# Step one of a two-step Fourier transform on TensorE: 128-row products with a zero-padded table against 64-row products per channel half

## The chip, the cores and the metric

The kernel runs on one core of one Trainium2 chip. A core has a matrix engine (TensorE, "PE" in the profile, with its weight loads as "PEld"), a vector engine (VectorE, DVE), a scalar engine (ScalarE, ACT), GpSimd (POOL) and a sync engine (SP) that here only issues DMAs. The engines run their own instruction streams and wait for each other through semaphores. SBUF is the working memory, 128 partitions wide; TensorE writes its results to PSUM, eight banks of 512 fp32 values per partition.

The metric is the device time of one execution in microseconds (us). The kernel before took 699.45 us in the median of three runs (695.64 to 699.81).

## The reference, cut to what matters

An H3 block (with adaptive layer norm) is followed by a token-mixing MLP. The change touches only the long convolution of the H3 block:

```python
kv = k_shift * v                                    # (S, D), S = 2048, D = 640
kv_f = rfft(pad(kv, S));  kf_f = rfft(pad(ssm_k, S))
y = irfft(kv_f * kf_f)[:S] + kv * ssm_D
out = q * y
```

`k_shift` is a causal convolution over four tokens, done on VectorE and GpSimd. After the convolution come a second layer norm and the MLP (2048 to 1728 to 2048 over the token axis), which make up the larger part of the time.

## The kernel before, in words

The 640 channels are worked in five chunks of 128 (loop variable `c`, L511). Each chunk has two halves of 64 channels, called `h`; tokens are split as n = 32 n1 + n2, with n1 (64 values) on the partitions. So partitions 0 to 63 hold the 64 n1 of the first channel half and partitions 64 to 127 those of the second.

The transform of each chunk has two steps forward and two back:

- **step1** (L210): 64-point transform over n1. It is called for two sides, the signal (side 0, in tile `x`) and the filter (side 1, in tile `p`), and for four values of t, each with eight pairs of channels (`a`). One `pst` tile (two PSUM banks, 1024 columns) holds one t. ScalarE copies it into the spectrum tile `z` (L220). The stationary operand is a 128 x 64 slice of the data; the moving operand is a column block of the table F1 (L218).
- **f2** (L223): 32-point transform with twiddles, stationary w, moving `z`, eight groups g, two column halves of the array. The product of signal and filter spectrum follows on ScalarE (L237: copy of the filter part to `kt`), VectorE (L242, L244: products into `p`, through the helper L59) and GpSimd or VectorE (L250: sums into `y`).
- **i2** (L254) and **i1** (L273): the two inverse steps. i2 works on 32-row tiles of the array and is copied back into `z` by ScalarE (L271, four copies); i1 works on 64 x 64 tiles, four of them, and its result is multiplied on VectorE with the normalised query (`gate`, L302, writes `aux`).

Nothing is scheduled by a planner: the order of the program text is the order on each engine. For a middle chunk TensorE's order is: f2 of the eight groups; step1(0,0), step1(0,1) of the next chunk; i2(0); step1(0,2); i2(1); step1(0,3); i1(0); step1(1,0); i1(1); step1(1,1) to step1(1,3); then f2 of the next chunk. Chunk 0 is set up ahead of the loop (L486 to L492), and in the last chunk there is no step1. Between the f2 groups VectorE is given the short convolution of the chunk after next (`fill`, `dv`; tiles `tap`, `kt`, `x`) or, late, statistics for the second layer norm (L510, tile `sm`).

The `pst` tiles are a ring of three (`ring`, L67: slots 0, 1, 2), shared by step1, f2, i2 and i1; a fourth pair of banks is the tile `tap`. A product of TensorE in fp32 appears in the trace as two pairs of a weight load and a matmul: the 16 products written in one step1 call are 32 such pairs.

The tables come from `_constants` (L21). F1 has a row for each (h, n1) and, for cosine and sine, a column for each (k1, h); it is zero where the two h differ, so that one 128-row product gives both halves at once, side by side. The tables F1, V2 and a unit matrix are loaded together as `SM` (L454, 420 columns).

Of the kernel before, what the change touches and what calls it, by code (L numbers as in the profile page):

```python
# [11 lines left out]
AF = mybir.ActivationFunctionType  # L12
# [8 lines left out]
def _constants():  # L21


    n1, n2, k1, k2 = np.arange(64), np.arange(32), np.arange(64), np.arange(32)
    a = 2 * np.pi * ((1 + 4 * k1)[None, :] * n1[:, None] % 256) / 256
    f1 = np.zeros((2, 64, 2, 64, 2))
    for h in range(2):
        f1[h, :, 0, :, h], f1[h, :, 1, :, h] = np.cos(a), np.sin(a)
    ang = 2 * np.pi * ((1 + 4 * k1)[None, :, None] * n2[:, None, None] / 8192
                       + (k2[None, None, :] * n2[:, None, None] % 32) / 32)  # L30
    w2 = np.zeros((2, 32, 2, 64, 2, 2, 32))
    for c in range(2):
        w2[0, :, c, :, 0, c] = np.cos(ang)
        w2[1, :, c, :, 0, c] = -np.sin(ang)
        w2[0, :, c, :, 1, c] = np.sin(ang)
        w2[1, :, c, :, 1, c] = np.cos(ang)
    ang = 2 * np.pi * (k2[:, None] * n2[None, :] % 32) / 32
    c, s = np.cos(ang), np.sin(ang)
    v2 = np.tile(np.concatenate([c, -s, s, c], 1), (4, 1))
    ang = 2 * np.pi * ((1 + 4 * k1)[:, None, None] * (32 * n1[None, None, :] + n2[None, :, None]) % 8192) / 8192  # L40
    v1 = np.tile(np.stack([np.cos(ang), np.sin(ang)], 1).reshape(64, 4096) / 2048, (2, 1))
    sel = np.zeros((128, 128))
    sel[0, 0:64] = sel[1, 64:128] = 1
    small = np.concatenate([f1.reshape(128, 256), v2, np.eye(128)[:, 0:36], sel], 1)
    return {"small": small.astype(np.float32), "w2": w2.reshape(128, 8192).astype(np.float32),
            "v1": v1.astype(np.float32)}

# [2 lines left out]
def mixer_kernel(ctx: ExitStack, tc: tile.TileContext, q, k, v, shift_k, ssm_k, ssm_D, w1, b1, w2, b2, c,  # L50
# [24 lines left out]
    def dram(t, offset, ap):  # L75
        return bass.AP(tensor=t.tensor, offset=t.offset + offset, ap=ap)
# [15 lines left out]
    KT = [T_kt[:, 512 * i:512 * i + 512] for i in range(2)]  # L92
    TV = T_kt[:, 1024:1536].rearrange("p (n i) -> p n i", i=64)

    Z = T_z.rearrange("p (s k t a e) -> p s t a k e", s=2, k=128, t=4, e=2)
    T2 = T_z[:, 4096:8192].rearrange("p (a m e) -> p a m e", a=32, e=2)
    Y = T_y.rearrange("p (r i k) -> p r i k", r=2, i=32)
    W2 = [t.rearrange("p (k m) -> p k m", m=64) for t in T_w2]
    V1 = T_v1[:, 0:4096].rearrange("p (r n m) -> p r n m", r=2, n=32)
    SM = T_v1[:, 4096:4516]  # L100
    F1, V2, ID = SM[:, 0:256], SM[:, 256:384], SM[:, 384:420]
    TR, DR = T_rows[:, 0:256], T_rows[:, 512:576]

    PS_, PT, PW = T_t[:, 0:512], T_t[:, 512:1024], T_t[:, 1024:1280].rearrange("p (s i) -> p s i", s=4)
# [105 lines left out]
    def step1(side, t, later=False):  # L210

        ps = psum()
        for a in range(8):
            i = 8 * t + a
            lhs = KSP[:, i] if side else X.rearrange("p (i m) -> p i m", i=32)[:, i]
            o = 256 * (a // 2) + a % 2
            for ri in range(2):
                pe.matmul(ps[64 * ri:64 * ri + 64, o:o + 255:2], lhs, F1[:, 128 * ri:128 * ri + 128], start=True,  # L218
                          stop=True)
        evac = lambda: act.activation(Z[:, side, t], ps.rearrange("p (a k e) -> p a k e", a=4, e=2), AF.Copy)  # L220
        return evac if later else evac()

    def f2(g):  # L223

        ps = psum()
        for kk in range(8):
            k1 = 8 * g + kk
            for ri in range(2):
                for h in range(2):
                    o = 128 * kk + 64 * ri  # L230
                    rhs = bass.AP(tensor=T_z.tensor, offset=T_z.offset + 64 * k1 + 32 * h,
                                  ap=[T_z.ap[0], [4096, 2], [1, 32]])
                    pe.matmul(ps[64 * h:64 * h + 64, o:o + 64], W2[k1 // 32][:, 2 * (k1 % 32) + ri], rhs, start=True, stop=True)  # L233
        pv = ps.rearrange("p (m s i) -> p m s i", s=2, i=32)
        xs_ = pv[:, :, 0]
        kt = KT[g % 2]
        act.activation(kt.rearrange("p (m i) -> p m i", i=32), pv[:, :, 1], AF.Copy)  # L237
        pa, pb = P[:, 1024 * (g % 2):1024 * (g % 2) + 512], P[:, 1024 * (g % 2) + 512:1024 * (g % 2) + 1024]
        m16 = lambda t: t.rearrange("p (m i) -> p m i", i=32)

        def mul():
            TT(dve, m16(pa), xs_, m16(kt), ALU.mult)  # L242
            sw = bass.AP(tensor=kt.tensor, offset=kt.offset + 32, ap=[kt.ap[0], [64, 8], [-32, 2], [1, 32]])
            TT(dve, pb.rearrange("p (k r i) -> p k r i", k=8, r=2), xs_.rearrange("p (k r) i -> p k r i", r=2), sw,  # L244
               ALU.mult)

        def add(eng=pool):
            for ri, t, op in ((0, pa, ALU.subtract), (1, pb, ALU.add)):
                t = t.rearrange("p (k r i) -> p r k i", k=8, r=2)
                TT(eng, Y[:, ri, :, 8 * g:8 * g + 8].rearrange("p i k -> p k i"), t[:, 0], t[:, 1], op)  # L250
        return mul, add
# [199 lines left out]
        load_k(0, g, both)  # L451
    for g in (0, 2, 1, 3):
        load_v(0, g, both)
    sync.dma_start(SM, dram(c_small, 0, [[548, 128], [1, 420]]))  # L454
    load_ks(0, act)

    def all_taps():
# [680 lines left out]
```

## Time and profile before

| | before |
|---|---|
| median of three runs | 699.45 us |
| the profiled execution, its own time | 697.86 us |
| its span, first to last instruction | 696.1 us |
| PE busy | 622.0 us (89%), 9099 matmuls, 9099 weight loads |
| DVE busy | 496.1 us (71%) |
| ACT busy | 291.6 us (42%) |
| POOL busy | 128.2 us (18%) |
| mean granted TensorE clock | 0.975 |
| step1 matmuls (L218), both sides | 39.6 + 39.7 us, 640 + 640 |
| f2 matmuls (L233) | 79.0 us, 2560 |
| copies of step1's result (L220) | 43.0 us, 40 |

A "pair" below is one weight load with its matmul, as the trace counts them. A row of the timeline gives the start and the length in us, the engine, the line, the operation, output <- inputs, the shapes, and how many instructions were merged; the bracket at the end is the idle time just before, and what ended it. "issue" there means that the engine waited for nothing that the profile shows. In a row of groups the numbers after the bar are the busy time in us, the mean length of one in ns, and the idle time before them.

The trace falls into the set-up with chunk 0 (to about 97 us), the chunk loop (to about 296 us), and the MLP (the rest). The change touches the first two.

### The profile page before, as it was taken

Reading aid. Unit: us, or ns where it says so; the run is one execution under the profiler, and the core shown is the slowest. Engines: PE = TensorE matmul, PEld = TensorE weight load, DVE = VectorE, ACT = ScalarE, POOL = GpSimd, SP = SyncE. Lnnn points to the kernel's source line nnn. Section 1 sums busy time; section 2 is a strip of 40 time slices with the busy share of each in tenths; the row PEclk is TensorE's granted clock in tenths of the full one; section 3 lists DMA queues with packets and bytes.
Section 4 is the critical chain, followed back from the end, with each engine's and each line's share of the span. In section 5 each row is a group of like instructions: output and inputs, shape, how many; then the busy total and the mean of one; then the engine's idle time right before and its main releaser. Section 6 shows DMA issues by size and latency. Waiting matters only on the chain.

```text
span 696.1 us, 20691 instructions
## 1 busy us (share of the span) xinstructions
PE 622.0 (89%) x9099; PEld 595.8 (86%) x9099; DVE 496.1 (71%) x866; ACT 291.6 (42%) x464; POOL 128.2 (18%) x147
## 2 busy tenths in 40 slices
PE   0689777898998988888899999999999989999997
PEld 0688466788988888778899979999999989999997
DVE  6769448978979449888985741123499868888986
ACT  0444373554746536456666232232244233233331
POOL 5184018513425025000100000000000430000000
PEclk9999798999999999999999999999999999999999
DMA  9988988627443424171305604433353533466611
GB/s 183 243 227 232 381 169 178 145 43 155 91 79 111 145 64 121 59 153 32 60 1 91 121 2 99 84 61 64 110 141 104 167 121 99 121 173 172 167 44 38
DMA packets 166930, 84.37 MB, mean 121 GB/s; under 512 B 91030, under 2 KB 157368, under 8 KB 166840
## 3 DMA queue, kind: packets, MB, share of 16 engines
q1 hardware_dynamic: 162292, 81.74, 46.9%
q10 hardware_dynamic: 4548, 1.31, 1.1%
q8 instruction: 71, 1.16, 0.7%
q14 instruction: 19, 0.16, 0.1%
HBM read 72.55 MB, written 10.49 MB: 119 GB/s over the span
## 4 chain that ended last, share of the span: by engine, by line
PE 62%; DVE 17%; DMA 6%; ACT 5%; SPq 4%; issue 3%; POOL 1%; ACTq 0%; POOLq 0%; DVEq 0%
PE pst L436 20%; PE pst L997 17%; PE pst L1074 7%; PE pst L218 5%; PE pst L233 4%; PE pst L262 4%; SPq L496 3%; DVE tap L59 3%; PE pst L282 2%; DVE p L59 2%; DMA aux<-in_A_ssm_k_dram 2%; DVE kt L59 2%; DMA w<-in_const_w_dram 1%; DMA aux<-in_w_mod_dram 1%; DVE aux L59 1%
## 5 line engine op out<-in xcount | busy, mean ns | idle before, releaser
L233 PE MATMUL pst<-z,w 128*64 128x64 f32 x2560 | 79.0, 223 | 12.0 <-ACT z L220 5.7
L233 PEld LDWEIGHTS pst<-z,w 128*64 128x64 f32 x2560 | 76.8, 138 | 14.8 <-issue 7.7
L220 ACT ACTIVATE z<-pst 128x1024 f32<-128x1024 f32 x40 | 43.0, 1076 | 51.4 <-PE pst L218 51.3
L218 PE MATMUL pst<-v,x 128*64 128x128 f32 x640 | 39.6, 282 | 27.2 <-DVE x L59 24.1
L218 PEld LDWEIGHTS pst<-v,x 128*64 128x64 f32 x640 | 36.9, 142 | 28.1 <-POOL t L459 23.6
L59 DVE TENSOR_TENSOR p<-pst,kt 128x512 f32<-128x512 f32 x80 | 50.9, 680 | 12.7 <-ACT kt L237 9.3
L59 POOL TENSOR_TENSOR y<-p 128x256 f32<-128x256 f32 x72 | 51.1, 744 | 38.8 <-DVE p L59 38.6
L218 PE MATMUL pst<-v,p 128*64 128x128 f32 x640 | 39.7, 283 | 6.8 <-DVE aux L59 4.6
L997 PE MATMUL pst<-r_z,m_w 128*128 128x320 f32 x222 | 42.1, 312 | 2.2 <-DVE m_w L59 2.2
L218 PEld LDWEIGHTS pst<-v,p 128*64 128x64 f32 x640 | 37.2, 143 | 8.0 <-DVE aux L59 4.9
L262 PEld LDWEIGHTS pst<-v,y 32*128 32x128 f32 x1280 | 39.7, 194 | 3.8 <-issue 2.6
L237 ACT ACTIVATE kt<-pst 128x512 f32<-128x512 f32 x40 | 23.9, 599 | 43.7 <-PE pst L233 30.1
L262 PE MATMUL pst<-v,y 32*128 32x64 f32 x1280 | 41.6, 279 | 0.7 <-ACT z L220 0.6
L833 ACT ACTIVATE pst<-pst,sm 128x640 f32<-128x640 f32 x13 | 10.0, 767 | 75.8 <-PE pst L436 75.8
L985 ACT ACTIVATE m_w<-m_v 128x896 fp32r<-128x896 f32 x24 | 22.7, 951 | 37.0 <-PE pst L997 16.8
L997 PEld LDWEIGHTS pst<-r_z,m_w 128*128 128x128 f32 x222 | 35.2, 190 | 2.4 <-DVE m_w L59 2.4
L59 DVE TENSOR_TENSOR tap<-tap,kt 128x512 f32<-128x512 f32 x51 | 35.5, 696 | 1.3
L59 DVE TENSOR_TENSOR kt<-in,tap 128x512 f32<-128x512 f32 x51 | 34.9, 685 | 1.4
L59 POOL TENSOR_TENSOR m_p<-u_i,r_z 128x320 f32<-128x320 f32 x1 | 0.9, 882 | 183.4 <-issue 183.4
L271 ACT ACTIVATE z<-pst 128x512 f32<-128x512 f32 x38 | 20.9, 646 | 21.9 <-PE pst L262 21.9
L59 DVE TENSOR_TENSOR m_w<-m_v,m_w 128x896 fp32r<-128x896 f32 x24 | 27.9, 1164 | 2.4 <-ACT m_w L985 1.9
L436 PE MATMUL pst<-r_z,wb0b 128*128 128x320 f32 x180 | 28.2, 310 | 0.9 <-DVE u_x L59 0.9
(289 smaller groups left out, 1445.0 us busy)
## 6 DMA issues: line engine op xcount, KB each, us to landing
x<-in_B_w_dram SPq DMA_DIRECT2D x20, 512.0 KB
aux<-in_A_ssm_k_dram SPq DMA_DIRECT2D x10, 512.0 KB
in<-in_A_k_dram SPq DMA_DIRECT2D x36, 128.0 KB
in<-in_A_v_dram SPq DMA_DIRECT2D x36, 128.0 KB
m_x<-xs SPq DMA_DIRECT2D x28, 160.0 KB
out_dram<-m_x SPq DMA_DIRECT2D x28, 160.0 KB
w<-in_const_w_dram SPq DMA_DIRECT2D x2, 2048.0 KB
m_v<-in_B_w_dram SPq DMA_DIRECT2D x9, 448.0 KB
```

What stands on the lines that cost most here:

```text
L59: TT = lambda eng, o, a, b, op: eng.tensor_tensor(o, a, b, op=op)
L218: pe.matmul(ps[64 * ri:64 * ri + 64, o:o + 255:2], lhs, F1[:, 128 * ri:128 * ri + 128], start=True, stop=True)
L220: evac = lambda: act.activation(Z[:, side, t], ps.rearrange("p (a k e) -> p a k e", a=4, e=2), AF.Copy)
L233: pe.matmul(ps[64 * h:64 * h + 64, o:o + 64], W2[k1 // 32][:, 2 * (k1 % 32) + ri], rhs, start=True, stop=True)
L237: act.activation(kt.rearrange("p (m i) -> p m i", i=32), pv[:, :, 1], AF.Copy)
L262: pe.matmul(pp[qd // 2][:, o:o + 64], Y[p, ri, i:i + 2].rearrange("p i k -> p (i k)"), V2[p, 64 * ri:64 * ri + 64], start=ri == 0, stop=ri ...
L271: act.activation(o, i, AF.Copy)
L436: pe.matmul(ps[0:m, h, 0:320], w_.bitcast(F32R), r_[:, 320 * h:320 * h + 320].bitcast(F32R), start=first and i == 0, stop=last and i == 2)
L496: sync.dma_start(XH[j // 8][64 * b:64 * b + 64, j % 8], dram(q, (16 * b + j) * D, [[32 * D, 64], [1, D]]))
L985: act.activation(W[n][0].bitcast(F32R), A[p, w_], AF.Copy)
L997: pe.matmul(bank[n], w[:, i].bitcast(F32R), r.bitcast(F32R), start=i == 0 and k == 0, stop=i == 6 and k == 2)
L1074: pe.matmul(acc[s][:, h, 0:320], w[:, f_].bitcast(F32R), u[r + h].bitcast(F32R), start=f_ == 0 and k == 0, stop=f_ == NF - 1 and k == 2)
```

## The change

F1 loses its zero blocks: it is now the same 64 x 128 table (cosine, sine) for both channel halves, one copy on partitions 0 to 63 and one on 64 to 127. step1 makes a product for each half by itself: 64 rows, 64 stationary columns, 64 moving columns. The four products of one `a` (two halves, cosine and sine) use four different quarters of the array; the halves go to the two PSUM banks of the tile, cosine and sine to its two partition halves. Each t has 32 written products in place of 16, each with half the moving columns.

The order of the columns in the `pst` tile changes with that: the half is now outermost, (h, a, k1, parity) in place of (a, k1, h, parity). ScalarE copies it with one instruction as before, and so the half lands inside the tile index of `z`: for one k1 and one half, f2's moving operand was one run of 32 values for each side, and is now four runs of 8 values, 16 apart. The `z` write has pairs of neighbouring values as before, 64 values apart in place of 32. The table load has 292 columns in place of 420.

```diff
-    f1 = np.zeros((2, 64, 2, 64, 2))
-    for h in range(2):
-        f1[h, :, 0, :, h], f1[h, :, 1, :, h] = np.cos(a), np.sin(a)
+    f1 = np.tile(np.concatenate([np.cos(a), np.sin(a)], 1), (2, 1))
...
-    Z = T_z.rearrange("p (s k t a e) -> p s t a k e", s=2, k=128, t=4, e=2)
+    Z = T_z.rearrange("p (s k t a e) -> p s t a k e", s=2, k=64, t=4, e=2)
...
-    SM = T_v1[:, 4096:4516]
-    F1, V2, ID = SM[:, 0:256], SM[:, 256:384], SM[:, 384:420]
+    SM = T_v1[:, 4096:4388]
+    F1, V2, ID = SM[:, 0:128], SM[:, 128:256], SM[:, 256:292]
...
-            o = 256 * (a // 2) + a % 2
+            o = 128 * (a // 2) + a % 2
             for ri in range(2):
-                pe.matmul(ps[64 * ri:64 * ri + 64, o:o + 255:2], lhs, F1[:, 128 * ri:128 * ri + 128], start=True,
-                          stop=True)
-        evac = lambda: act.activation(Z[:, side, t], ps.rearrange("p (a k e) -> p a k e", a=4, e=2), AF.Copy)
+                for h in range(2):
+                    r = slice(64 * h, 64 * h + 64)
+                    pe.matmul(ps[64 * ri:64 * ri + 64, 512 * h + o:512 * h + o + 127:2], lhs[r],
+                              F1[r, 64 * ri:64 * ri + 64], start=True, stop=True)
+        evac = lambda: act.activation(Z[:, side, t], ps.rearrange("p (a k e) -> p a k e", a=8, e=2), AF.Copy)
...
-                    rhs = bass.AP(tensor=T_z.tensor, offset=T_z.offset + 64 * k1 + 32 * h,
-                                  ap=[T_z.ap[0], [4096, 2], [1, 32]])
+                    rhs = bass.AP(tensor=T_z.tensor, offset=T_z.offset + 64 * k1 + 8 * h,
+                                  ap=[T_z.ap[0], [4096, 2], [16, 4], [1, 8]])
...
-    sync.dma_start(SM, dram(c_small, 0, [[548, 128], [1, 420]]))
+    sync.dma_start(SM, dram(c_small, 0, [[420, 128], [1, 292]]))
```

More of the change, by code (lines that the diff above doesn't have):

```diff
@@ L43, in _constants @@
     sel[0, 0:64] = sel[1, 64:128] = 1
-    small = np.concatenate([f1.reshape(128, 256), v2, np.eye(128)[:, 0:36], sel], 1)
+    small = np.concatenate([f1, v2, np.eye(128)[:, 0:36], sel], 1)
     return {"small": small.astype(np.float32), "w2": w2.reshape(128, 8192).astype(np.float32),
```

## The prediction

> **What bounds the kernel now.** I read the page first, then the table of stretches (`A:B` in us, then busy time and instruction count of each engine, granted clock, DMA share, GB/s), then TensorE's timeline from 20 to 296 us.
>
> ```profile
> span 696.1 us, 20691 instructions
> q8 instruction: 71, 1.16, 0.7%
> L220 ACT ACTIVATE z<-pst 128x1024 f32<-128x1024 f32 x40 | 43.0, 1076 | 51.4 <-PE pst L218 51.3
> ```
> ```profile
> 0.00:38.00 38.00, 14.41 (x229) 14.45 (x231) 28.40 (x46) 9.90 (x9) 13.34 (x17) 1.00 1.03 208
> 38.00:97.00 59.00, 48.32 (x1168) 40.59 (x1168) 34.72 (x82) 24.20 (x39) 22.56 (x26) 0.88 0.89 270
> 164.80:181.00 16.20, 15.94 (x516) 15.60 (x518) 15.90 (x26) 9.56 (x22) 9.48 (x15) 1.00 0.57 134
> ```
>
> Up to 97 us the DMA engines are full (shares 1.03 and 0.89); step1 of chunk 0 lies there, and making it faster brings nothing. After about 296 us there is no step1. Between, TensorE is nearly always busy, but in f2 so is VectorE (15.94 and 15.90 of 16.20 us from 164.8). So step1's time counts in full only where VectorE waits for TensorE.
>
> **The price of step1.** Rows of TensorE's timeline:
>
> ```profile
> 126.16 2.09 PE L233 MATMUL pst<-z,w 128*64 128x64 f32 x64 [1.15 <-DVE p L59]
> 134.46 3.71 PE L218 MATMUL pst<-v,x 128*64 128x128 f32 x64 [0.44 <-DVE p L59]
> 150.12 2.10 PE L282 MATMUL pst<-z,v 64*64 64x64 f32 x128 [0.19 <-ACT z L271]
> 153.75 1.53 PE L218 MATMUL pst<-v,p 128*64 128x128 f32 x24 [0.95 <-issue]
> 155.21 1.75 PE L282 MATMUL pst<-z,v 64*64 64x64 f32 x104
> 157.75 0.58 PE L282 MATMUL pst<-z,v 64*64 64x64 f32 x24 [0.80 <-issue]
> 158.26 5.46 PE L218 MATMUL pst<-v,p 128*64 128x128 f32 x96
> ```
>
> One t of step1 is 32 pairs and takes 3.71 / 2 = 1.85 us (58 ns a pair). After the change it is 64 pairs of 64x64 on four quarters of the array. Exactly this form stands in i1 (L282): 128 pairs in 2.10 us, 16.4 ns each, so one t would take 1.05 us, 0.8 less. Bounds: 16.4 ns, and the 32.7 ns of f2 (64 pairs in 2.09 us), whose quarters cannot overlap by rows; I take i1's. [...]
>
> **But the same rows show a second price.** The two "issue" gaps at L282 lie 24 + 104 = 128 pairs apart. The page says why that number: 71 packets of 1.16 MB are 16.3 KB each, and 9099 weight loads plus 9099 matmuls over 71 packets are 256 instructions, 128 pairs. So TensorE runs out of instructions at the packet's edge. From one resumption to the next, (153.75 to 157.75) a packet took 4.00 us; the other places:
>
> ```profile
> 47.85 3.95 PE L233 MATMUL pst<-z,w 128*64 128x64 f32 x127 [0.28 <-issue]
> 52.17 3.95 PE L233 MATMUL pst<-z,w 128*64 128x64 f32 x127 [0.37 <-issue]
> 196.42 2.10 PE L282 MATMUL pst<-z,v 64*64 64x64 f32 x128 [0.20 <-ACT z L271]
> 198.45 2.00 PE L218 MATMUL pst<-v,p 128*64 128x128 f32 x32
> 200.38 2.31 PE L282 MATMUL pst<-z,v 64*64 64x64 f32 x128
> 202.62 5.46 PE L218 MATMUL pst<-v,p 128*64 128x128 f32 x96
> 242.84 0.44 PE L218 MATMUL pst<-v,x 128*64 128x128 f32 x3 [0.94 <-issue]
> 243.20 2.08 PE L282 MATMUL pst<-z,v 64*64 64x64 f32 x124
> 246.39 0.33 PE L282 MATMUL pst<-z,v 64*64 64x64 f32 x4 [1.10 <-issue]
> 250.84 5.46 PE L218 MATMUL pst<-v,p 128*64 128x128 f32 x96
> ```
>
> 3.55 us (242.84 to 246.39) and 4.32 us (47.85 to 52.17): a packet needs 3.55 to 4.3 us when it is asked for back to back, against 2.10 us in which 128 pairs of 64x64 use it up. Old step1 used one in 7.4 us and gave the supply time; new step1 runs as fast as i1. In the stretch from 196.42, 288 pairs pass in 6.27 us without a gap, so somewhat over one packet lies ready. My estimate for a long stretch of 64x64 pairs: 16.4 ns each, plus a first gap of 1.3 us and 1.5 us (3.6 - 2.1) for each further packet.
>
> **The change, part by part.** A middle chunk goes from 1280 pairs to 1536. In order:
>
> *Table, 64 KB less of DMA* (128 columns x 128 rows): 0.3 us at the 208 GB/s of the first stretch; two more packets of instructions there take half back: -0.2.
>
> *Chunk 0's last two t.*
>
> ```profile
> 108.42 5.87 PE L218 MATMUL pst<-v,p 128*64 128x128 f32 x64 [4.65 <-DVE aux L59]
> 118.22 1.29 DVE L59 TENSOR_TENSOR p<-pst,kt 128x512 f32<-128x512 f32 x2 [1.98 <-ACT kt L237]
> 92.32:95.80 3.48, 3.48 (x132) 3.48 (x136) 1.53 (x2) 1.09 (x2) 0.00 (x0) 0.51 0.98 156
> 108.42:112.20 3.78, 3.78 (x36) 3.78 (x38) 3.61 (x6) 0.05 (x1) 3.62 (x3) 0.50 0.80 165
> ```
>
> The granted clock is 0.50 there. i1 at 92.32 had 0.51 and passed 132 pairs in 3.48 us, 26.4 ns each, so 128 pairs take 3.4 us in place of 5.87, with packets ready after an idle 4.65 us. f2 starts over 2 us earlier, VectorE waited 1.98 for it, and is full from there on: -2.0.
>
> *Chunks 1 to 3, start: step1(0,0..1) then i2.* i2 needs Y, VectorE's last sums.
>
> ```profile
> 136.62 1.06 DVE L59 TENSOR_TENSOR y<-p 128x256 f32<-128x256 f32 x2
> 138.10 3.80 PE L262 MATMUL pst<-v,y 32*128 32x64 f32 x128
> 226.94 1.06 DVE L59 TENSOR_TENSOR y<-p 128x256 f32<-128x256 f32 x2
> 228.63 1.10 ACT L220 ACTIVATE z<-pst 128x1024 f32<-128x1024 f32 x1 [2.23 <-PE pst L218]
> 230.27 3.88 PE L262 MATMUL pst<-v,y 32*128 32x64 f32 x128
> ```
>
> In chunk 1 Y is ready at 137.68, so i2 can gain 0.4 at most; chunk 2 is alike. In chunk 3 Y is ready at 228.0, and the ring's slot after a copy of 1.10 that now starts 0.8 earlier, at 228.9: 1.4, of which I take 1.2.
>
> *step1(0,2), step1(0,3)* lie beside ScalarE's copies after i2:
>
> ```profile
> 141.93 2.25 ACT L271 ACTIVATE z<-pst 128x512 f32<-128x512 f32 x4 [0.69 <-PE pst L262]
> ```
>
> i2(1) waits for these copies, 2.25 us, longer than one t of 1.85, before the change and after: 0. Were this cover gone, the two would be worth 0.8 each.
>
> *From i1(0) to the end of i1(1)*, which releases VectorE's second gate. Before: 128 + 32 + 128 pairs, 8.2 us in chunk 1 (150.12 to 158.33), 6.27 in chunk 2, 7.65 in chunk 3 (243.20 to 250.85). After: 320 pairs, 5.25, and one gap of 1.3: 6.6. Differences -1.6, +0.3, -1.0.
>
> *step1(1,1..3)*, 192 pairs at the end of the same stretch. From i1(0) there are 512 pairs: 8.4 + 1.3 + 2 x 1.5 = 12.7 us, against 13.6, 11.66 and 13.1. So f2 starts 0.9 earlier, 1.0 later and 0.4 earlier, its own share beside the start.
>
> ```profile
> 168.85 1.28 DVE L59 TENSOR_TENSOR p<-pst,kt 128x512 f32<-128x512 f32 x2
> 211.36 0.60 ACT L237 ACTIVATE kt<-pst 128x512 f32<-128x512 f32 x1 [2.18 <-PE pst L233]
> 213.20 1.28 DVE L59 TENSOR_TENSOR p<-pst,kt 128x512 f32<-128x512 f32 x2
> 260.26 1.29 DVE L59 TENSOR_TENSOR p<-pst,kt 128x512 f32<-128x512 f32 x2 [4.41 <-ACT kt L237]
> ```
>
> Behind chunk 1, f2 keeps both engines full, so the smaller gain counts: -0.4 - 0.9 = -1.3. Behind chunk 2, VectorE is late (kt lies ready at 211.96, the product starts at 213.20), which hides f2's later start; its gate counts: -0.4 + 0.3 = -0.1. Behind chunk 3, VectorE waits 4.41 us for f2, so f2's start counts: -1.2 - 0.4 = -1.6.
>
> *f2's moving operand in runs of 8:* 0. i1 moves runs of two values (T2, L283) at 16.4 ns. *ScalarE's copy, pairs 64 values apart:*
>
> ```profile
> L59 DVE TENSOR_TENSOR x<-tap,in 128x512 f32<-128x512 f32 x17 | 11.7, 689 | 8.5 <-PE pst L218 8.1
> L59 DVE TENSOR_TENSOR kt<-in,tap 128x512 f32<-128x512 f32 x51 | 34.9, 685 | 1.4
> L59 DVE TENSOR_TENSOR y<-p 128x256 f32<-128x256 f32 x8 | 4.3, 612 | 0.0
> ```
>
> The write to `x` has that same pattern and costs 689 against 685 ns in a run: 0. Upper end: `y`, single values 64 apart, 612 ns for 256, twice the rate per value; a copy of 1.08 would become at most 2.2, +3 a chunk. No wait is added and no DMA moved past another.
>
> **Sum:** -0.2 - 2.0 - 1.3 - 0.1 - 1.6 = -5.2. The profiled execution took 697.86 (its span 696.1 and 1.8 around it) and would take 692.7; the median of the runs is 1.6 above it, 699.45, so I forecast 694.2. My choices of gap sizes give it 690 to 698.
>
> **Rivals.**
>
> *A, the supply keeps up* (0.16). No gaps: gate earlier by 8.2 - 5.25, 1.0 and 2.4; behind chunk 3 only ScalarE's three copies (3 x 1.06) follow, and f2 starts about 4.6 earlier. -0.2 - 2.0 - (0.4 + 3.0) - (0.4 + 1.0) - (1.2 + 4.6) = -12.8: 686.7. Against it: gaps of 0.80 to 1.10 us exist with half the step1 pairs. [...]
>
> *B, the supply is worse* (0.14). Each packet takes 4.3 us as at 47.85, and less lies ready: first gap 1.9, further ones 2.2. Until gate 9.3 us: +1.1, +3.0, +1.6; f2 behind chunk 3 +1.6. -2.2 + 0.7 + 2.6 + 0.4: +1.5, 701.0.
>
> *C, the four quarters don't run together* (0.14): the change doesn't do what it says, because output columns two apart or the order of quarters serialises them. Then f2's 32.7 ns holds, one t takes 2.09, +0.24 each: 3 on the path in chunks 1 and 2, 6 in chunk 3, 2 in chunk 0: +3.4, and a gap of 0.3 at some edges: +4, 703.5. It decides from 29 ns a pair.
>
> *D, f2's reads are slow* (0.09), the case on the other side: runs of 8 cost as `y` does, 0.4 ns a value more ((612 - 512) / 256), 13 ns a pair with two halves at once. f2 would take 2.9 in place of 2.09 us a group: over 20 us in chunks 1 to 4, less VectorE's slack of some 5, with the forecast +10 to +15: 712. It decides when a group needs about 2.3 us.
>
> **How the numbers follow.** Forecast 0.47, A 0.16, B 0.14, C 0.14, D 0.09. 1% is 7 us, about what a measurement of this kernel tells from no change, so the borders lie at 692.5 and 706.4. Faster: most of A and a quarter of the forecast, 0.28; slower: D and the upper part of C, 0.15; same 0.57. The range leaves out half of A and all of D: 687 to 705.
>
> **What would show it.** L218 with 2560 rows in 64x64 form, about 16 ns a pair outside gaps, 27 or more at half clock; "issue" gaps 128 pairs apart in every stretch from i1(0) to f2, 1.0 to 1.9 us; L220 still 1076 ns; f2 still 2.1 us a group; VectorE's wait of 1.98 in chunk 1 gone. The prediction is wrong if no such gaps appear (A), if L218 shows 30 ns a pair (C), or if f2's groups lengthen (D).

## The result, and the profile after

The change made the kernel slower. After: 720.18 us (median of four, 718.06 to 725.34); before, beside it: 699.32 us (median of four, 695.64 to 699.81). The ratio is 1.032, with a 95% interval of 1.0255 to 1.0387. The forecast was 694.2 with a range of 687 to 705, so the sign was wrong and the time lies 15 us outside the range. The profiled execution took 718.06 us against 697.86, 20.2 us more, with a mean granted clock of 0.926 against 0.975.

From the page of after, the lines that answer to those of before (the span, the busy time of each engine, and the queue that brings instructions):

```profile
span 716.3 us, 23255 instructions
PE 622.8 (87%) x10379; PEld 596.2 (83%) x10379; DVE 496.3 (69%) x866; ACT 290.1 (41%) x464; POOL 128.9 (18%) x147
q8 instruction: 81, 1.33, 0.8%
```

TensorE has 1280 pairs more (10379 against 9099) and needs ten packets of instructions more (81 against 71). Its busy time has hardly moved (622.8 against 622.0), although step1 became cheaper. The groups of after show what took its place:

```profile
L262 PE MATMUL pst<-v,y 32*128 32x64 f32 x1280 | 59.4, 354 | 3.5 <-ACT z L220 2.5 <-DVE y L57 0.6 <-issue 0.4
L218 PE MATMUL pst<-v,x 64*64 64x64 f32 x1280 | 29.1, 258 | 31.9 <-DVE x L57 23.7 <-issue 6.4 <-ACT kt L237 1.3
L218 PE MATMUL pst<-v,p 64*64 64x64 f32 x1280 | 26.0, 239 | 17.4 <-issue 13.5 <-DVE aux L57 3.8
```

step1 (L218) went from 79.3 us (39.6 + 39.7) to 55.1, so 24 us of work are gone. But 19.9 us of idle time (6.4 + 13.5) are put down to "issue" ahead of it, that is, to no wait that the profile shows; and i2 (L262), which the change doesn't touch, went from 41.6 us in the same 1280 matmuls to 59.4. Its group of before:

```profile
L262 PE MATMUL pst<-v,y 32*128 32x64 f32 x1280 | 41.6, 279 | 0.7 <-ACT z L220 0.6
```

Where the time went is read from the starts of the stages on TensorE's timeline. Before (those that the prediction doesn't show):

```profile
115.45 9.55 PE L233 MATMUL pst<-z,w 128*64 128x64 f32 x320 [1.17 <-ACT z L220]
143.73 4.30 PE L262 MATMUL pst<-v,y 32*128 32x64 f32 x128
164.87 16.13 PE L233 MATMUL pst<-z,w 128*64 128x64 f32 x512 [1.15 <-ACT z L220]
184.43 3.80 PE L262 MATMUL pst<-v,y 32*128 32x64 f32 x128
209.23 7.68 PE L233 MATMUL pst<-z,w 128*64 128x64 f32 x256 [1.15 <-ACT z L220]
257.43 11.45 PE L233 MATMUL pst<-z,w 128*64 128x64 f32 x384 [1.12 <-ACT z L220]
274.83 0.45 PE L233 MATMUL pst<-z,w 128*64 128x64 f32 x6 [1.40 <-issue]
```

After:

```profile
113.83 8.32 PE L233 MATMUL pst<-z,w 128*64 128x64 f32 x269 [1.18 <-ACT z L220]
136.00 0.84 PE L262 MATMUL pst<-v,y 32*128 32x64 f32 x10 [0.54 <-ACT z L220]
137.27 4.60 PE L262 MATMUL pst<-v,y 32*128 32x64 f32 x118 [0.42 <-issue]
143.71 7.51 PE L262 MATMUL pst<-v,y 32*128 32x64 f32 x128
153.09 3.69 PE L282 MATMUL pst<-z,v 64*64 64x64 f32 x128
168.17 0.45 PE L233 MATMUL pst<-z,w 128*64 128x64 f32 x8 [1.18 <-ACT z L220]
188.47 0.44 PE L262 MATMUL pst<-v,y 32*128 32x64 f32 x4 [0.57 <-DVE y L57]
208.16 3.48 PE L282 MATMUL pst<-z,v 64*64 64x64 f32 x128
221.67 0.33 PE L233 MATMUL pst<-z,w 128*64 128x64 f32 x2 [1.17 <-ACT z L220]
243.60 5.50 PE L262 MATMUL pst<-v,y 32*128 32x64 f32 x128
260.29 3.16 PE L282 MATMUL pst<-z,v 64*64 64x64 f32 x126
275.81 15.15 PE L233 MATMUL pst<-z,w 128*64 128x64 f32 x448 [1.11 <-ACT z L220]
294.84 0.45 PE L233 MATMUL pst<-z,w 128*64 128x64 f32 x6 [1.68 <-issue]
```

| mark | before | after | later by | added since the mark before |
|---|---|---|---|---|
| first f2 starts | 115.45 | 113.83 | -1.6 | -1.6 |
| i2(0) of chunk 1 | 138.10 | 136.00 | -2.1 | -0.5 |
| i1(0) of chunk 1 | 150.12 | 153.09 | 3.0 | **5.1** |
| f2 behind chunk 1 | 164.87 | 168.17 | 3.3 | 0.3 |
| i2(0) of chunk 2 | 184.43 | 188.47 | 4.0 | 0.7 |
| i1(0) of chunk 2 | 196.42 | 208.16 | 11.7 | **7.7** |
| f2 behind chunk 2 | 209.23 | 221.67 | 12.4 | 0.7 |
| i2(0) of chunk 3 | 230.27 | 243.60 | 13.3 | 0.9 |
| i1(0) of chunk 3 | 243.20 | 260.29 | 17.1 | **3.8** |
| f2 behind chunk 3 | 257.43 | 275.81 | 18.4 | 1.3 |
| its last matmul ends | 275.28 | 295.29 | 20.0 | 1.6 |

So 16.5 of the 20 us arise between i2(0) and i1(0) (the bold rows), where the change removed work. The table of stretches says why (columns: length, then busy time and count of PE, PEld, DVE, ACT and POOL, the granted clock, DMA share, GB/s). After:

```profile
139.60:156.70 17.10, 17.10 (x437) 16.60 (x431) 8.14 (x8) 6.36 (x10) 0.00 (x0) 0.50 0.09 23
170.30:173.70 3.40, 3.40 (x72) 3.40 (x68) 3.30 (x6) 1.36 (x3) 0.31 (x1) 0.50 0.50 114
190.80:211.30 20.50, 20.39 (x489) 19.85 (x488) 9.34 (x10) 7.14 (x11) 0.00 (x0) 0.50 0.33 55
245.40:262.50 17.10, 17.10 (x412) 16.60 (x411) 2.02 (x4) 7.63 (x11) 0.00 (x0) 0.50 0.29 65
```

and before, from i2(0) of chunk 1 to f2:

```profile
138.10:164.80 26.70, 23.61 (x706) 22.13 (x704) 20.28 (x25) 13.62 (x16) 4.75 (x2) 1.00 0.39 74
```

All three i2 stages of after fall to half clock (0.50 in the first, third and fourth of these rows, against 1.00 before): the second call of i2 in chunk 1 takes 7.51 us (row at 143.71) instead of 4.30 (row of before at 143.73). f2 behind chunk 1 has a half-clock stretch of 3.40 us too (0.50 from 170.30), and there is one more in f2 behind chunk 3 (0.50 from 276.10 to 279.50). The reader is to see that in these stretches TensorE is busy practically all the time (17.10 of 17.10 us in two of them, 20.39 of 20.50 in the third): the "busy" column of the page hides the loss, and only the clock column beside it tells.

### The profile page after: what moved, and what is told of

It reads as the page before. It is cut to its first block, busy times and chain, and to the rows that moved or that the text cites. A ratio compares the mean times of both kernels' runs of the same rounds, so it can differ in the third digit from the quotient of the medians.

```text
span 716.3 us, 23255 instructions
## 1 busy us (share of the span) xinstructions
PE 622.8 (87%) x10379; PEld 596.2 (83%) x10379; DVE 496.3 (69%) x866; ACT 290.1 (41%) x464; POOL 128.9 (18%) x147
## 4 chain that ended last, share of the span: by engine, by line
PE 62%; DVE 14%; SPq 6%; DMA 6%; issue 5%; ACT 4%; POOL 2%; ACTq 0%; DVEq 0%; POOLq 0%
PE pst L436 19%; PE pst L997 17%; PE pst L1074 7%; PE pst L262 7%; PE pst L233 5%; PE pst L218 3%; SPq L496 3%; PE pst L282 3%; DVE p L57 2%; DVE tap L57 2%; DMA w<-in_const_w_dram 1%; DMA aux<-in_w_mod_dram 1%; DMA in<-in_A_k_dram 1%; DVE kt L57 1%; SPq L149 1%
## 5 line engine op out<-in xcount | busy, mean ns | idle before, releaser
L233 PE MATMUL pst<-z,w 128*64 128x64 f32 x2560 | 82.4, 227 | 13.2 <-ACT z L220 5.8
L233 PEld LDWEIGHTS pst<-z,w 128*64 128x64 f32 x2560 | 80.1, 142 | 15.5 <-issue 8.8
L57 DVE TENSOR_TENSOR p<-pst,kt 128x512 f32<-128x512 f32 x80 | 51.0, 683 | 16.9 <-ACT kt L237 16.4
L262 PEld LDWEIGHTS pst<-v,y 32*128 32x128 f32 x1280 | 57.4, 265 | 6.1 <-issue 4.8
L262 PE MATMUL pst<-v,y 32*128 32x64 f32 x1280 | 59.4, 354 | 3.5 <-ACT z L220 2.5
L220 ACT ACTIVATE z<-pst 128x1024 f32<-128x1024 f32 x40 | 41.4, 1060 | 51.7 <-PE pst L218 51.7
L218 PE MATMUL pst<-v,x 64*64 64x64 f32 x1280 | 29.1, 258 | 31.9 <-DVE x L57 23.7
L218 PEld LDWEIGHTS pst<-v,x 64*64 64x64 f32 x1280 | 26.8, 169 | 33.5 <-issue 31.3
L997 PE MATMUL pst<-r_z,m_w 128*128 128x320 f32 x222 | 42.2, 313 | 2.2 <-DVE m_w L57 2.2
L218 PE MATMUL pst<-v,p 64*64 64x64 f32 x1280 | 26.0, 239 | 17.4 <-issue 13.5
L218 PEld LDWEIGHTS pst<-v,p 64*64 64x64 f32 x1280 | 24.1, 154 | 18.5 <-issue 14.5
L997 PEld LDWEIGHTS pst<-r_z,m_w 128*128 128x128 f32 x222 | 35.3, 191 | 2.4 <-DVE m_w L57 2.4
L282 PE MATMUL pst<-z,v 64*64 64x64 f32 x1280 | 27.3, 248 | 7.5 <-issue 5.1
L282 PEld LDWEIGHTS pst<-z,v 64*64 64x64 f32 x1280 | 25.6, 163 | 9.6 <-issue 6.2
```

Source lines behind the costliest of these rows:

```text
L57: TT = lambda eng, o, a, b, op: eng.tensor_tensor(o, a, b, op=op)
L218: pe.matmul(ps[64 * ri:64 * ri + 64, 512 * h + o:512 * h + o + 127:2], lhs[r], F1[r, 64 * ri:64 * ri + 64], start=True, stop=True)
L262: pe.matmul(pp[qd // 2][:, o:o + 64], Y[p, ri, i:i + 2].rearrange("p i k -> p (i k)"), V2[p, 64 * ri:64 * ri + 64], start=ri == 0, stop=ri ...
L282: pe.matmul(ps[64 * b:64 * b + 64, 512 * e + 64 * jj:512 * e + 64 * jj + 64], V1[p, ri, n2], T2[p, :, 32 * ri + n2], start=ri == 0, stop=r ...
L997: pe.matmul(bank[n], w[:, i].bitcast(F32R), r.bitcast(F32R), start=i == 0 and k == 0, stop=i == 6 and k == 2)
```

## The experiments

Two causes were weighed: the **granted clock**, if it falls when the work of the array gets thin, and the **supply of instructions**, which has to bring twice as many pairs for step1. Beside them stood the new layout of the spectrum (case D of the prediction). The ratios are against the kernel before on the same chip.

### e4: the layout alone

```diff
-    f1 = np.zeros((2, 64, 2, 64, 2))
+    f1 = np.zeros((2, 64, 2, 2, 64))
-        f1[h, :, 0, :, h], f1[h, :, 1, :, h] = np.cos(a), np.sin(a)
+        f1[h, :, 0, h], f1[h, :, 1, h] = np.cos(a), np.sin(a)
...
-        evac = lambda: act.activation(Z[:, side, t], ps.rearrange("p (a k e) -> p a k e", a=4, e=2), AF.Copy)
+        evac = lambda: act.activation(Z[:, side, t], ps.rearrange("p (a k e) -> p a k e", a=8, e=2), AF.Copy)
...
-                    rhs = bass.AP(tensor=T_z.tensor, offset=T_z.offset + 64 * k1 + 32 * h,
-                                  ap=[T_z.ap[0], [4096, 2], [1, 32]])
+                    rhs = bass.AP(tensor=T_z.tensor, offset=T_z.offset + 64 * k1 + 2 * h,
+                                  ap=[T_z.ap[0], [4096, 2], [4, 16], [1, 2]])
```

This is the kernel before, with its 128-row products, and the half inside the tile index of `z`. f2 reads runs of two values, shorter even than the runs of eight of the change.

> The kernel before with the layout of the spectrum alone changed: products of 128 rows and 128 columns as before, the half inside the tile index of z, f2 reading runs of two values, four apart (finer than the change's runs of eight), ScalarE writing pairs 64 values apart. Both theories: f2 at 2.1 us a group, the copy at 1.08 us, 697 to 701 us. If reading or writing z in short runs costs (the prediction's case D): f2's group above 2.3 us and 705 us or more.

Measured: 699.88 us, ratio 0.9996 (0.9958 to 1.0034). The groups of e4:

```profile
L233 PE MATMUL pst<-z,w 128*64 128x64 f32 x2560 | 79.4, 220 | 13.9 <-ACT z L220 5.7 <-issue 4.9 <-DVE p L59 3.1
```

f2 needs 79.4 us in all, where before it needed 79.0. The layout costs nothing that shows (the interval reaches from -0.4 to +0.3%), so the loss has to come from the products of step1.

### e1: the same number of products, with 128 rows

```diff
-    f1 = np.tile(np.concatenate([np.cos(a), np.sin(a)], 1), (2, 1))
+    f1 = np.zeros((2, 64, 2, 128))
+    for h in range(2):
+        f1[h, :, h] = np.concatenate([np.cos(a), np.sin(a)], 1)
...
-                    r = slice(64 * h, 64 * h + 64)
+                    r = slice(0, 128)
...
-                              F1[r, 64 * ri:64 * ri + 64], start=True, stop=True)
+                              F1[r, 128 * h + 64 * ri:128 * h + 64 * ri + 64], start=True, stop=True)
```

This is the kernel after with as many products, but each takes all 128 rows with the zero-padded table. The count of instructions stays; the array is used by more rows and for longer (31 ns a pair, below).

> The changed kernel with one thing undone: every product of step1 takes all 128 rows again (table zero-padded, 64 moving columns, one product per half), so it has the changed kernel's number of products, its banks and its layout of z, but only two quarters at a time. Theory 'clock' (the 64-row products leave too little activity around i2, the granted clock halves and i2 takes twice as long): i2 back at 3.8 us per call in chunks 1 to 3, granted clock there 1.0, step1 2.1 us per t, time 700 to 705 us. Theory 'supply' (the added instructions cost the 20 us, since 12 packets a chunk are needed in place of 10): the number of instructions is unchanged, so 712 to 722 us.

Measured: 714.64 us, ratio 1.0189 (1.0098 to 1.0281), with a clock of 0.964 in the profiled execution. In chunk 1 a call of i2 took 4.1 us, and in chunk 2 the calls took 3.79 us (124 pairs) and 4.22 (2.22 and 2.00 with a gap between), but the step1 behind the second took 3.65 us (at 204.81) where the same 64 pairs took 2.13 in chunk 1. i2 itself was slow in chunk 3 alone, in its first call (clock 0.50 from 245.80 to 256.00). TensorE's timeline of e1 there:

```profile
245.30 0.27 PE L220 MATMUL pst<-v,x 128*64 128x64 f32 x1 [1.94 <-issue]
245.50 6.90 PE L264 MATMUL pst<-v,y 32*128 32x64 f32 x128
```

The time is the one expected from "supply", i2's calls are mostly as expected from "clock". With wider products i2 keeps its 3.8 to 4.2 us a call in two chunks of three, and the kernel still loses some 13 us (0.0189 of 699). e1 doesn't separate what of that is the count of products: its pairs take 31 ns (128 of them 3.97 us, at 140.49), so that one t needs 1.99 us in place of 1.85, and in its profiled execution (718.35 us, the longest of the four) f2 of chunk 0 starts 6.0 us later than before (121.49 against 115.45), for a reason that stays open. In chunk 3 the order of events can be seen: a gap of 1.94 us that is put down to "issue", and then i2 at a clock of 0.50 (6.90 us).

### e2 and e3: one side each with 128 rows

The edit is that of e1, with `r` depending on the side.

```diff
-                    r = slice(64 * h, 64 * h + 64)
+                    r = slice(0, 128) if side == 0 else slice(64 * h, 64 * h + 64)
```

(e2; in e3 `side == 1`). Only side 0 stands beside i2.

> The changed kernel with 128-row products for side 0 alone (the calls that stand around i2), 64-row products for side 1 (the calls around and after i1). Clock: i2 at 3.8 us per call, granted clock 1.0 around it; the gaps of instruction supply from i1 to f2 stay at 1 to 2 us each; 699 to 705 us. Supply: the gaps stay and so does the loss, 712 to 720 us.

> The opposite: 64-row products for side 0 alone, 128-row products for side 1. Clock: i2 still at 5.5 to 7.5 us per call in chunks 1 to 3, 713 to 720 us, although the gaps between i1 and f2 go. Supply: without those gaps 699 to 704 us.

Measured: e2 712.3 us, ratio 1.0182 (1.0107 to 1.0257); e3 721.51 us, ratio 1.031 (1.024 to 1.038). i2's group of e2:

```profile
L264 PE MATMUL pst<-v,y 32*128 32x64 f32 x1280 | 41.2, 277 | 3.6 <-issue 3.0 <-ACT z L222 0.6
```

With wide products on side 0, i2 is back at 41.2 us (before 41.6); in e3, with wide products on side 1 alone, it stays at 55.9 (after 59.4). So the products beside i2, on side 0, matter for i2's time, and those of side 1 don't bring it back. It is no fixed rule: in chunk 2 of e3 the calls of i2 passed 124 pairs in 3.79 and 3.86 us beside the same 64-row products, and so they did in chunk 2 of e6 below (3.79 and 3.86 us). TensorE's timeline of e3:

```profile
195.12 3.79 PE L264 MATMUL pst<-v,y 32*128 32x64 f32 x124 [1.25 <-ACT z L222]
201.10 3.86 PE L264 MATMUL pst<-v,y 32*128 32x64 f32 x124 [0.58 <-ACT z L273]
```

Neither time is the one expected from "clock" (699 to 705 us for e2, 713 to 720 for e3); e2's is the one expected from "supply" (712 to 720). e2, in which i2 is healed, is still 12.7 us slower than before. Its wide pairs on side 0 take 44.4 us where before took 39.6 (64 pairs behind i2 of chunk 3 that took 3.49 us, in place of 2.13, included), and in its profile the three stretches from i1(0) to f2 are 6.0 us longer than before in all. e2's timeline ahead of f2 behind chunk 1 shows one of them:

```profile
159.92 1.03 PE L284 MATMUL pst<-z,v 64*64 64x64 f32 x54 [1.91 <-issue]
163.92 3.37 PE L220 MATMUL pst<-v,p 64*64 64x64 f32 x120 [1.91 <-issue]
```

TensorE comes back 4.00 us later, has worked through its 128 pairs in 2.1, and waits the other 1.9. Behind the gaps the clock is low (0.53 from 163.92 to 167.30): the 120 pairs from 163.92 take 3.37 us, 28 ns each instead of 17.

### e5: filler products beside i2

```diff
-    def step1(side, t, later=False):
+    def step1(side, t, later=False, fill_pe=False):
...
+        if fill_pe:
+            pe.matmul(ps[:, 0:512], T_w2[0][:, 0:128], T_w2[0][:, 0:512], start=True, stop=True)
...
-            step1(0, 2)
+            step1(0, 2, fill_pe=True)
```

(The same for `step1(0, t)` and `step1(0, 3)`.) The kernel after, with one full-array product ahead of each step1 of side 0 in chunks 1 to 3, whose result is overwritten. It adds work and takes nothing away.

> The changed kernel with work added: each of step1(0,0) to step1(0,3) in chunks 1 to 3 begins with one product of 128 rows, 128 stationary and 512 moving columns of the table w, whose result is overwritten at once (2 pairs, about 0.9 us). It brings TensorE's array time per t back to about that of the kernel before, with hardly an instruction more. Clock: granted clock around i2 back at 1.0, i2 at 3.8 us a call, 701 to 707 us although work was added. Supply: the number of instructions is the changed kernel's, and 4 x 0.9 us a chunk come on top where they are not hidden: 719 to 726 us.

Measured: 711.9 us, ratio 1.0174 (1.0109 to 1.024); after stood at 1.0321. TensorE's timeline of e5:

```profile
138.52 3.80 PE L264 MATMUL pst<-v,y 32*128 32x64 f32 x128
150.48 2.10 PE L284 MATMUL pst<-z,v 64*64 64x64 f32 x128
153.94 1.10 PE L220 MATMUL pst<-v,p 64*64 64x64 f32 x61 [1.37 <-issue]
157.94 1.15 PE L284 MATMUL pst<-z,v 64*64 64x64 f32 x62 [1.91 <-issue]
161.95 3.69 PE L220 MATMUL pst<-v,p 64*64 64x64 f32 x128 [1.29 <-issue]
166.79 7.94 PE L235 MATMUL pst<-z,w 128*64 128x64 f32 x256 [1.15 <-ACT z L222]
216.51 16.23 PE L235 MATMUL pst<-z,w 128*64 128x64 f32 x496 [1.14 <-ACT z L222]
268.42 12.97 PE L235 MATMUL pst<-z,w 128*64 128x64 f32 x384 [1.12 <-ACT z L222]
```

Twelve fillers of 1.1 us were added, and the kernel became 8 us faster: i2(0) takes 3.80 us again, and from i2(0) to i1(0) it is 11.96 us (138.52 to 150.48), as before the change, with a clock of 1.00 (138.52 to 148.40); in chunks 2 and 3 the calls of i2 take 4.03 to 4.31 us. That shows half clock around i2 as a cause of the loss. It doesn't tell what triggers it, since the gap ahead of i2 in chunk 1 (0.42 us in after) is gone here too. The size was missed: 701 to 707 us had been expected, so the supply had been taken too small. With i2 at 3.80 to 4.31 us a call, the way from i1(0) to f2 is 16.3 us in chunk 1 (150.48 to 166.79) against 14.75 before (150.12 to 164.87), and the gaps of 1.37, 1.91 and 1.29 us are its reason, together with the half clock among them (0.50 from 159.20 to 166.00; 3.69 us for the last 128 pairs).

The same rows can be set against the supply for a whole chunk. A chunk of after is 1536 pairs, 12 packets of 128. Before the change, with 10 packets, a chunk took 44.4 us (164.87 to 209.23) and 48.2 (209.23 to 257.43). In e5 it took 49.7 (166.79 to 216.51) and 51.9 (216.51 to 268.42), 4.1 and 4.3 us per packet: close to the 4.0 us in which TensorE comes back when it waits for nothing else (153.94, 157.94, 161.95). That would fit a supply which limits the whole chunk, but it isn't shown: the fillers add array time of their own, and in the chunk from 166.79 TensorE is idle for instructions for 6.6 us between i1(0) and f2 (1.72, 1.91, 1.36, 1.63) and for 0.45 us elsewhere.

### e6 and e7: without the loads

```diff
     def load_k(c, g, engs=(sync, sync)):
+        if c > 1:
+            return
```

(the same in `load_v`, `load_halo` and `load_ks`; e6 is the kernel after, e7 the kernel before). The question is whether the packets of instructions are slow because they share the DMA engines with the loads.

> The changed kernel without the input loads of chunks 2 to 4 (k, v and the filter; the transforms work on what chunk 1 left, so the output is not the reference's). The packets of instructions then meet nearly empty DMA queues in the loop. Supply: gaps of 1 to 2 us shrink below 0.8 us, 705 to 712 us. Clock alone, with the gaps no cause of it: i2 still at 5.5 us or more per call, 714 to 720 us. If the gaps are what lowers the clock: both vanish, 697 to 702 us.

> The control: the kernel before without the same loads (output not the reference's for the same reason). Its five gaps of 0.8 to 1.4 us shrink; 693 to 698 us. What the loads cost beside the gaps shows here too.

Measured: e6 713.34 us, ratio 1.0188 (1.0102 to 1.0275); e7 697.4 us, ratio 0.9967 (0.9929 to 1.0005). TensorE's timeline of e6 in chunk 3:

```profile
263.80 1.21 PE L290 MATMUL pst<-z,v 64*64 64x64 f32 x67 [0.91 <-issue]
267.80 2.09 PE L226 MATMUL pst<-v,p 64*64 64x64 f32 x128 [1.86 <-issue]
```

The gaps and the 4.00 us between two resumptions (263.80 to 267.80) stay without the loads, where gaps below 0.8 us had been expected if the supply gained from it. In e7 too they are hardly smaller (up to 1.95 us). So contention with these loads doesn't make a packet's 4 us (other transfers remain: the DMA share is 0.24 from 256 to 276), and most of the change's loss is still there (713.34 against 697.4). The wait stands uncovered where 128 pairs are used up in 2.09 us (from 267.80): TensorE then waits 1.91 us, to 271.80.

### e8: less work beside i2

```diff
-        for a in range(8):
+        for a in range(4 if half else 8):
...
-            step1(0, 2)
+            step1(0, 2, half=True)
```

(The same for `step1(0, t)` and `step1(0, 3)`.) The kernel before, with its 128-row products, but half of step1's products left out on side 0 in chunks 1 to 3; ScalarE copies the first bank twice. It tells whether the form of the products is needed for the loss, or only that there is less work.

> The kernel before with half of step1's side 0 left out in the making of chunks 1 to 3: four of eight channel pairs per t, 16 pairs of instructions in place of 32, the copy takes the computed bank twice (output not the reference's). Less work and fewer instructions, all of it 128 rows. Clock: the windows around i2 fall below what keeps the clock, i2 at 5.5 to 7.5 us a call, 706 to 718 us. Supply: fewer packets, 694 to 699 us.

Measured: 704.71 us, ratio 1.0109 (1.0014 to 1.0203). TensorE's timeline of e8 in chunk 1, and the stretch in which the clock is halved:

```profile
141.40 0.89 PE L267 MATMUL pst<-v,y 32*128 32x64 f32 x23 [1.14 <-issue]
143.84 7.80 PE L267 MATMUL pst<-v,y 32*128 32x64 f32 x128
```
```profile
142.60:156.20 13.60, 13.58 (x258) 12.60 (x258) 6.05 (x5) 6.14 (x12) 0.00 (x0) 0.50 0.04 8
```

Twelve calls with half the products, some 11 us less for the array (12 times half of 1.85), and the kernel does not get faster; the interval lies just on the slower side, and the time lies between what "supply" (694 to 699 us) and "clock" (706 to 718 us) had led to expect. i2(1) of chunk 1 takes 7.80 us although no product has 64 rows. So the form of 64 rows isn't needed to lose the clock (0.50 in the row above). Less work isn't always enough either: in chunk 2 of e8 the calls of i2 took 4.10 us and, for 124 pairs, 3.79, and in chunk 3 the stretch of 0.50 (241.60 to 248.40) begins only in the second call, behind a gap of 0.74 us.

### e9: side 1 alone with 64 rows

```diff
+                if side == 1:
+                    for h in range(2):
+                        r, o2 = slice(64 * h, 64 * h + 64), 512 * h + 128 * (a // 2) + a % 2
+                        pe.matmul(ps[64 * ri:64 * ri + 64, o2:o2 + 127:2], lhs[r],
+                                  F1[r, 128 * ri + h:128 * ri + 128:2], start=True, stop=True)
```

The kernel before, with side 1 changed and side 0 as it was. It keeps the wide products beside i2 and doubles the products where they follow one another closely.

> The kernel before with 64-row products in side 1 alone (around and after i1), old layout of z; its copy is two instructions of 512 columns, about 0.1 us more each t. Side 0 and the instructions around i2 are those of before. Supply: i2 at 3.8 us a call and 1.0 clock around it, but from i1(0) to f2 gaps of 1.3 to 2 us, 16 to 17 us in chunks 1 to 3 against 14.7, 12.8 and 14.2: 704 to 709 us. If the clock around i2 were the whole loss: 695 to 700 us.

Measured: 706.05 us, ratio 1.0079 (1.0053 to 1.0105). The calls of i2 keep their time (3.80 and 4.26 us in chunk 1; 40.7 us in all). TensorE's timeline of e9:

```profile
159.53 1.05 PE L295 MATMUL pst<-z,v 64*64 64x64 f32 x57 [3.00 <-issue]
```

Here the loss is some 6 us, as expected of the supply. In the profile the three stretches from i1(0) to f2, with gaps of up to 3.00 us, are 2.7 us longer than before in all, f2 behind chunk 3 is 2.0 us longer, and 1.2 us arise beside i2 of chunk 3: after a gap of 0.35 us inside i2, the step1 behind it, with its wide products as before, took 3.60 us (at 239.24) for the 32 pairs that took 1.97 in chunk 1.

### e10: side 0 alone with 64 rows, and the filler

The edit of e9 for `side == 0`, with the filler of e5. If a version with a gain was to be had from the change, this one was to be it.

> The kernel before with 64-row products in side 0 alone, each of these calls in chunks 1 to 3 begun with the one large product that the filler run had, old layout of z, two copies; side 1 is that of before. Both causes are then away: i2 at 3.8 us, gaps as before, 698 to 703 us. If the 64-row form cost something else (its copy, its banks), 706 us or more.

Measured: 706.47 us, ratio 1.009 (1.0055 to 1.0124), where 698 to 703 had been expected: a miss. The profiled execution took 711.79 us, more than most of the eight runs. In its chunks 1 and 2 i2 kept its time (3.8 to 4.5 us a call); in chunk 3 it did not (6.09 and 7.10 us). TensorE's timeline of e10:

```profile
238.32 0.69 PE L223 MATMUL pst<-v,x 64*64 64x64 f32 x29 [2.27 <-issue]
238.93 6.09 PE L277 MATMUL pst<-v,y 32*128 32x64 f32 x128
255.91 2.08 PE L214 MATMUL pst<-w 128*128 128x512 f32 x2
```

A gap of 2.27 us precedes the halving, as one of 1.94 does in e1. The clock is 0.50 from 240.10 to 260.60, with two fillers in that stretch, which take 2.08 us each in place of 1.13. So the filler does not make sure of the clock.

### e11 and e12: filler where before itself runs at half clock

The prediction showed that step1(1,2..3) of chunk 0 runs at half clock (0.50) after an idle time of 4.65 us. Both kernels are the one before, with four overwritten full-array products into that idle time; e11 also puts twenty ahead of the second MLP product (L997).

```diff
+            if c == 0 and t == 1:
+                warm = psp.tile([128, 1024], F32, name="warm0", tag=f"pst{ring[s10]}", bufs=1)
+                for _ in range(4):
+                    pe.matmul(warm[:, 0:512], T_w2[0][:, 0:128], T_w2[0][:, 0:512], start=True, stop=True)
```
```diff
+        if n == 0:
+            for _ in range(20):
+                pe.matmul(bank[n], U[0][0][:, 0:128], U[0][0], start=True, stop=True)
```

(The first in both, the second in e11 alone.)

> The kernel before with nothing of the change, only TensorE kept busy in two of its waits with products whose result is overwritten: four of 128x128x512 behind step1(1,1) of chunk 0, and twenty of 128x128x320 ahead of the last stage (L997), where TensorE is idle for 15 us. Clock: step1(1,2..3) of chunk 0 in 3.7 in place of 5.9 us, the first 3.4 us of the last stage at full clock: 695 to 697.5 us where before has 699. If TensorE's activity doesn't set the clock: 699.

> The kernel before with the four overwritten products behind step1(1,1) of chunk 0 alone. The twenty ahead of the last stage are left away: their place was misread, TensorE ran products there that only the list of the longest pieces had hidden, and they cost 8 us. Clock: f2 of chunk 1 starts 2 to 2.5 us earlier, 695.5 to 697.5 us. If what is won there is given back by f2's wait for VectorE: 699.

Measured: e11 707.29 us, ratio 1.0112 (1.0083 to 1.014), a miss: TensorE is not idle ahead of L997, and the twenty products stand on the path with 9.85 us. e12 695.7 us (median of 12), ratio 0.9955 (0.993 to 0.9981). TensorE's timeline of e12:

```profile
109.32 3.71 PE L218 MATMUL pst<-v,p 128*64 128x128 f32 x64
114.18 9.55 PE L233 MATMUL pst<-z,w 128*64 128x64 f32 x320 [1.15 <-ACT z L220]
```

With the array kept busy, the clock is 1.00 from 106.10 to 112.90, where before had 0.50; the same 64 pairs take 3.71 us instead of 5.87, and f2 starts at 114.18 instead of 115.45. e12 is the fastest kernel of this study, by 0.45% against before: little, but its interval does not reach 1. In this place, where the change was forecast to gain 2.0 us, four products with no use gain 1.3. A further 1.5 us in the profile lie between i1(0) and f2 of chunk 1, where the "issue" gaps are 0.43 us in place of 0.95 and 0.80; whether the four products brought that about stays open.

## Why the prediction was wrong

**What held.** The price of step1's pair: 64 pairs of 64x64 in 1.10 us at a clock of 1.00 (211.48 to 212.58),

```profile
211.48 1.10 PE L218 MATMUL pst<-v,p 64*64 64x64 f32 x64
```

17 ns a pair against the 16.4 taken, so case C fell. ScalarE's copy: 1060 ns against 1076, and f2's reads (e4), so case D fell. (Case D's 0.4 ns a value was taken from 512 ns, which no row shows; the rows of 612 ns for 256 values and 685 for 512 give about 1.05 ns.) Chunk 0: f2 starts 1.6 us earlier against 2.0 forecast, and VectorE's product follows at 116.88 without its wait of 1.98 us.

The "issue" gaps were foretold in every stretch from i1(0) to f2, and there they are, 3.5 to 4.3 us from one resumption to the next. But after has others that the prediction put at nothing, among them 0.67 us in f2 (at 169.29) and 2.05 us ahead of i2 of chunk 3 (at 243.40).

**The step that failed: "start: step1(0,0..1) then i2", and "step1(0,2), step1(0,3) ... 0".** Both took i2's 3.8 us a call from the trace of before and carried it over. The forecast was -0.4, -0.4 and -1.2 for the starts and 0 for what lies between i2(0) and i1(0); the starts gave -0.5, and then +0.7 and +0.9 for f2 and start together, and between i2(0) and i1(0) came +5.1, +7.7 and +3.8. The trace of before had the warning: in the quoted stretches i1 passed 132 pairs in 3.48 us where the clock was 0.51, and step1 took 5.87 us at 0.50, after an idle time. The prediction used these rows to price chunk 0 and did not ask whether its own change would bring the same state elsewhere. "Were this cover gone, the two would be worth 0.8 each" looked at the cover by ScalarE and not at what the wide products did for the clock: e8, which takes half of them away, loses it in chunk 1 (0.50 from 142.60 to 156.20).

**The term that was mis-sized: the supply, "a first gap of 1.3 us and 1.5 us (3.6 - 2.1) for each further packet".** From i1(0) to f2 the forecast was -0.9, +1.0 and -0.4; after has +0.3, +0.7 and +1.3. The gaps there, 4.3 us by the forecast, are 4.1, 2.7 and 4.9 us in after. That looks near, but I take it for luck: a half-clock i2 uses a packet in 7.5 us, which would give the supply time. In e5, where i2 takes 3.80 to 4.31 us a call, the gaps are 4.6, 6.6 and 7.1 us, and the stretches are longer than before by 1.6, 3.6 and 2.7; and in e2 and e9 time is lost there with i2 at 41.2 and 40.7 us in all. The failed thought, as far as the rows show it, is that the supply counts only behind i1(0). Where TensorE waits for it, a packet comes in about 4.0 us (e5: 153.94, 157.94, 161.95); f2 uses one in 4.2 us (two groups of 2.09) and i2 in 3.8, so by this reading neither lets the supply get far ahead, and old step1, with a packet in 7.4 us, was the part of the chunk in which it could catch up. Case B had gaps of about the size that e5 shows (1.9 and twice 2.2 us), but no half clock, and so too small a price (701).

**How the two hang together.** The halvings beside i2 that are shown above have a gap shortly before them: 0.42 us ahead of i2 at 137.27 in after (0.50 from 139.60), 1.14 to 141.40 in e8 (0.50 from 142.60), 1.94 to 245.30 in e1 (0.50 from 245.80), 2.27 to 238.32 in e10 (0.50 from 240.10). Gaps don't always do it: before has gaps of 0.95 and 0.80 us among wide step1 products, ending at 153.75 and 157.75, and its clock stays at 1.00 (row of before's stretch, to 164.80). What the clock follows is not shown. In chunk 1 more work for the array beside i2 brought it back (e5: 1.00 from 138.52 to 148.40, where after fell to 0.50 from 139.60) and less work lost it (e8). But chunk 2 of e3, e6 and e8 speaks against a simple rule: thin products and idle times of 0.3 to 1.3 us stand beside i2 there, and its calls took 3.8 to 4.1 us. What decides in the single case stays open. e5 shows that the clock around i2 is worth at least the 8 us that came back, e2 that up to 12.7 us are lost without it, by gaps, the half clock behind them and the array time of its wide pairs. They don't add up, since slow i2 hides gaps and gaps may bring on the slow i2; how the 21 us split stays open.

## What to carry to other kernels

Before splitting a product into smaller tiles, count the instruction packets that a pass of the loop then needs and set their time (here 4.0 us for 128 pairs) against the pass; where the array's time per packet comes out shorter than that, the time saved may turn into waiting, as here behind i1(0) (gaps of 4.6, 6.6 and 7.1 us in e5). And look at the granted clock beside the neighbours of the shortened stage, since it can fall there, as i2's did here (41.6 us before, 59.4 after, 41.2 again in e2): a busy TensorE at half clock looks like a busy TensorE in every column but one.

## What the runs showed of the hardware

- The clock halved here with no long idle time ahead of it. In after 17.10 of 17.10 us are busy at a clock of 0.50 from 139.60 to 156.70, and the idle times ahead of that were 0.54 us (at 136.00) and 0.42 us (at 137.27). The five half-clock stretches of after named above lasted 3.40, 3.40, 17.10, 17.10 and 20.50 us.
- Less work was no faster here, and by its interval slightly slower (e8: ratio 1.0109, from 1.0014, with half of step1's side 0 gone in chunks 1 to 3), and useless work faster (e5 by 8 us against after; e12 by 4.0 us against before beside it, 695.7 against 699.68).
- Where TensorE waits for instructions, a packet (256 of them: 2 x 10379 over 81 packets in after) came about every 4.0 us, whether the loads of chunks 2 to 4 run (e5: 153.94, 157.94, 161.95) or not (e6: 263.80, 267.80); single distances are 3.5 to 4.3 us.
